# Fused linear attention and SoLU MoE layer on one core: two-bank PSUM rooms with 1024-column instructions, another load order, and a new order of the work

## The chip, the core and the metric

The kernel runs on one core of a Trainium2 chip. The metric is the device time of one execution in microseconds (us). Three runs of the kernel before gave 177.38, 177.45 and 177.94 us; their median, 177.45 us, is what the change is measured against.

## What is computed

The reference takes q, k and v of shape (8 batches, 8 heads, 576 positions, 64 channels) and two weight matrices:

```python
kv  = einsum('bhsd,bhse->bhde', k, v)           # 64x64 per head
o   = einsum('bhsd,bhde->bhse', q, kv)
x   = o / sqrt(mean(o*o, -1) + 1e-6) * g_norm   # then reshaped to (4608 tokens, 512)
h   = x @ w_in                                  # 512 -> 1024
sm  = softmax(h);  u = h * sm
ln  = (u - mean(u)) / sqrt(var(u) + 1e-6) * g_ln
out = ln @ w_out                                # 1024 -> 512
```

The kernel forms u = h * exp(h) without the softmax's denominator, which falls out of the layer norm up to its epsilon; the sum of exp(h) enters through that epsilon alone. The mean over the channels is taken out of w_out beforehand (`w_center`), so a token's output is one matmul times one number per token (`rstd`).

## The kernel before

**Chunks.** The tokens are cut into nine chunks of 512. Chunks 0 to 7 hold eight of the nine positions per row of one batch; chunk 8 (`LAST`) holds the ninth positions of all batches. Each chunk runs through the same stages, and several chunks are in work at once:

- `kv_mm` (L368): k^T v of a batch, 64x64 matmuls on the four quadrants of TensorE (PE), into a PSUM room `kv`; `kv_copy` (L384) copies it to SBUF three times (`part` 0, 1, 2), because the product with q needs it in both partition halves. For batches 0 and 1 the heads come in two groups (second figure 0 or 1 in a piece's name), and the copies are made per group and per pair of heads.
- `qT`: q turned so that the channels lie on the partitions, for chunks 0 to 3 by PE (`qT_mm` L422, eight 128x128 transposes per half, then a copy), for chunks 4 to 8 (`XBAR`) by a DMA transpose that SyncE (SP) issues (`q_turn` L433).
- `o_mm` (L439) in two halves `hf` of four heads each, into two rooms of one bank (z = 0, 1); `sq` (L454) squares on ScalarE (ACT), one instruction of 512 columns per z; `oa` adds the two channel halves; `s_mm` (L462) sums over a head's channels; `ln` and `ex` give the reciprocal root; `x_mul` (L486) on VectorE (DVE) makes x with four instructions of 256 columns per half.
- `h_mm` (L530): eight blocks f of 128 channels, four matmuls (dt = 0 to 3) of 512 columns each, in a room of one bank; `h_exp` (L537) on ACT and `h_u` (L541) on DVE, 512 columns per instruction; `u_sq` (L545) squares u on GpSimd (POOL) or ACT; `e_sum` (L549) on POOL adds the two exponentials of a pair of blocks.
- `fold` (L569) on DVE halves u (`ua`), u squared (`usqa`) and the exponentials' sums (`esa`) `FOLDS` and `E_FOLDS` times; `sums` (L587) adds what is left on PE; `turn`, `stats` and `rstd` make the factor.
- `out_mm` (L649): four token blocks m, eight matmuls each; `scale` (`ob`) multiplies by `rstd`; `store` writes to DRAM. The last block of chunk 8 goes in two halves of 256 columns (L656).

**Order.** Nothing is scheduled by the compiler. `ORDER` (L20) is a list of pieces; `Plan.emit` (L150) issues them in that sequence, so each engine works its own pieces in the order of the list, and waits where an operand or a room is not ready. A suffix such as `:act` names the engine where there is a choice. `ROOMS` (L93) gives for each tile, when it is first used, the number of the PSUM bank or buffer that it gets. `Plan.run` (L122) adds three waits: the next POOL piece waits for DVE's folds and adds that stand before it in the list; a DMA transpose on SP waits for the load before the last one that POOL issued; and the next load that POOL issues waits for the DMA transposes before it.

**Loads.** The second group of k and v of batch 0 comes as fp32 through SP (`wide`) and is narrowed by ACT; all other loads of k, v, q and the weights are issued by POOL, with a cast to bf16. Before, the POOL queue carries q.0.1, v.0.0, k.0.0, q.0.0, v.1.0, k.1.0, q.1.0, w_in.0, w_in.1, q.1.1, v.1.1, k.1.1, w_out.0, w_out.1, q.2.0, k.2.0, v.2.0, q.3.0, v.3.0, k.3.0, q.4.0 and so on. Seven groups of matmuls on zeros (`warm`, L297; 27 in all) stand among the first pieces.

Of the kernel before, what the change touches and what calls it, by code (L numbers as in the profile page):

```python
# [19 lines left out]
ORDER = """  # L20
wide.v ident wide.k g_rows q.0.1 v.0.0 k.0.0 q.0.0 v.0.1:act v.1.0 k.1.0 q.1.0 w_in.0 k.0.1:act w_in.1 warm.0
kv_mm.0.1.0 qT_mm.0.1 kv.0.1.0.0:act kv.0.1.1.0 kv_mm.0.1.1 q.1.1 qT.0.1:act kv.0.1.2.1 kv.0.1.2.0 kv.0.1.1.1
kv.0.1.0.1:act warm.1 kv_mm.0.0.0 v.1.1 kv_mm.0.0.1 o_mm.0.1 kv.0.0.0.1 sq.0.1.1 warm.2 qT_mm.0.0 k.1.1 kv.0.0.1.0:act
kv.0.0.2.0:act kv.0.0.1.1:act kv.0.0.0.0:act qT.0.0 kv.0.0.2.1:act sq.0.1.0 warm.3 o_mm.0.0 w_out.0 turn_g sq.0.0.0
s_mm.0.1 g_mean sq.0.0.1 warm.4 kv_mm.1.0.1 w_out.1 ex.0.1 kv_mm.1.0.0 kv.1.0.2.1 s_mm.0.0 kv.1.0.2.0 kv.1.0.0.1:act
kv.1.0.0.0 kv.1.0.1.1 kv.1.0.1.0 qT_mm.1.0 ex.0.0 q.2.0 qT.1.0:act x.0.0.0 x.0.0.1 warm.5 o_mm.1.0 sq.1.0.0 warm.6
h.0.6.0 h.0.3.0 k.2.0 sq.1.0.1 x.0.1.0 table h.0.0.0 oa.1.0 x.0.1.1 s_mm.1.0 h.0.2.0 h.0.7.0 h.0.2.1 ln.1.0 v.2.0
ex.1.0 h.0.6.1 x.1.0.1 exp.0.6 q.3.0 h.0.3.1 exp.0.2 x.1.0.0 h.0.7.1 h.0.1.0 exp.0.7 u.0.6 v.3.0 qT_mm.1.1 h.0.0.1
exp.0.3 h.0.1.1 u.0.2 usq.0.6 h.1.2.0 exp.0.0 qT.1.1 kv_mm.1.1.1 exp.0.1 kv_mm.1.1.0 k.3.0 kv.1.1.0.1 h.0.4.0 h.0.4.1
u.0.1 kv.1.1.2.1:act kv.1.1.0.0:act es.0.0 kv.1.1.1.0:act kv.1.1.2.0:act kv.1.1.1.1 u.0.3 o_mm.1.1 exp.0.4 h.0.5.0  # L30
u.0.7 sq.1.1.0 es.0.3 h.0.5.1 u.0.4 sq.1.1.1 h.1.0.0 w_mean.0 usq.0.1:act oa.1.1 u.0.0 exp.0.5 s_mm.1.1 ln.1.1 ex.1.1
u.0.5 es.0.2 w_mean.1 w_mean.2 w_mean.3 w_mean.4 w_mean.5 w_mean.6 usq.0.5:act x.1.1.1 usq.0.2 usq.0.7:act w_mean.7
x.1.1.0 usq.0.0 q.4.0 usq.0.4:act w_center.5 h.1.3.0 qT_mm.2.1 h.1.7.0 w_center.1 h.1.4.0 h.1.7.1 qT.2.1:act q.5.0
w_center.4 h.1.0.1 v.4.0 w_center.0 exp.1.7 qT_mm.2.0 exp.1.0 w_center.3 h.1.1.0 h.1.1.1 k.4.0 qT.2.0:act w_center.2
h.1.2.1 es.0.1 u.1.7 h.1.3.1 exp.1.1 h.1.4.1 u.1.0 exp.1.3 out.0.2.0 es.1.0 usq.0.3 u.1.1 exp.1.2 out.0.2.1 kv_mm.2.0
w_center.7 exp.1.4 h.1.5.0 w_center.6 kv.2.1.0:act kv.2.0.0:act h.1.5.1 kv.2.0.2:act kv.2.1.1 kv.2.0.1:act es.1.1
u.1.4 out.0.2.2 kv.2.1.2:act exp.1.5 o_mm.2.0 u.1.3 o_mm.2.1 sq.2.0.1 out.0.2.3 usq.1.1 u.1.2 qT_mm.3.0 sq.2.0.0 u.1.5
out.0.0.0 sq.2.1.1 oa.2.0 out.0.0.1 sq.2.1.0 qT.3.0 s_mm.2.0 usq.1.5 out.0.0.2 ln.2.0 qT_mm.3.1 oa.2.1:pool ex.2.0
h.1.6.0 qT.3.1 out.0.0.3 usq.1.2:act x.2.0.0 x.2.0.1 h.1.6.1 s_mm.2.1 exp.1.6 sums.0 usq.1.7 ln.2.1 u.1.6 ex.2.1
kv_mm.3.0 es.1.2 turn.0 stats.0 out.0.3.0 kv.3.1.0:act x.2.1.0 x.2.1.1 usq.1.0:act out.0.3.1 usq.1.4 usq.1.3 h.2.6.0  # L40
out.0.3.2 rstd.0 h.2.0.0 ob.0.0:act usq.1.6 kv.3.0.1 ob.0.2 h.2.6.1 kv.3.1.2:act kv.3.0.0:act kv.3.1.1:act out.0.3.3
usqa.1.0 kv.3.0.2:act h.2.4.0 exp.2.6 h.2.5.0 ob.0.3:act ua.1.0 o_mm.3.0 h.2.1.0 store.0.3 sq.3.0.0 h.2.0.1 sq.3.0.1
u.2.6 h.2.1.1 store.0.0 exp.2.0 h.2.5.1 usqa.1.1 out.0.1.0 exp.2.1 oa.3.0 h.2.4.1 ua.1.1 exp.2.5 qT.4 s_mm.3.0
out.0.1.1 u.2.0 ln.3.0 es.1.3 out.0.1.2 u.2.5 h.2.7.0 ex.3.0 h.2.7.1 u.2.1 exp.2.4 es.2.0 h.2.3.0 x.3.0.1 exp.2.7
o_mm.3.1 sq.3.1.0 x.3.0.0 usq.2.6 out.0.1.3 sq.3.1.1 h.2.2.0 h.2.3.1 u.2.7 qT.5 ob.0.1:act h.2.2.1 oa.3.1 sums.1
exp.2.3 u.2.4 es.2.3 kv_mm.4.0 exp.2.2 u.2.3 store.0.1 usq.2.5:act s_mm.3.1 turn.1 es.2.2 out.1.3.0 kv.4.1.0
kv.4.0.1:act ln.3.1 u.2.2 store.0.2 out.1.3.1 kv.4.0.0 usq.2.7 ex.3.1 stats.1 out.1.2.0 kv.4.0.2:act kv.4.1.1 kv.4.1.2
rstd.1 x.3.1.1 usq.2.0 o_mm.4.0 o_mm.4.1 ob.1.3 sq.4.0.1 out.1.0.0 usq.2.4 x.3.1.0 sq.4.0.0 store.1.3 out.1.2.1
sq.4.1.0 oa.4.0 ua.2.0 sq.4.1.1 s_mm.4.0 out.1.0.1 ln.4.0 oa.4.1 h.3.2.0 ex.4.0 ob.1.0 v.5.0 s_mm.4.1 x.4.0.0 h.3.7.0
k.5.0 ln.4.1 x.4.0.1 exp.3.2 es.2.1 h.3.3.0 ex.4.1 u.3.2 h.3.6.0 exp.3.3 ua.2.1 exp.3.7 h.3.5.0 x.4.1.0 u.3.3 v.6.0  # L50
exp.3.6 x.4.1.1 h.3.1.0 exp.3.5 q.6.0 usq.2.2:act h.3.4.0 usq.3.3 ob.1.2:act usq.2.1:act usq.2.3:act exp.3.4 es.3.1
# [684 lines left out]
```

## Time and profile before

| what | value |
| --- | --- |
| median of three runs | 177.45 us |
| span of the profiled execution, first to last instruction | 175.8 us |
| profiled execution's own time | not listed apart; its span is 1.65 us less than the median |
| busy: PE, weight loads, DVE, ACT, POOL | 164.2, 80.3, 145.5, 152.1, 99.8 us |
| granted TensorE clock | 1.00 in every slice |
| first h matmul, end of the last output matmul | 19.84 and 172.5 us |

The span counts from the first instruction to the last. The profile has a page with busy times, groups of instructions and the chain that ended last; the trace behind it answers for a window of time, for one tile, and as a timeline in which runs of like instructions are merged (start, duration, engine, line, operation, how many, and in brackets how long the engine sat idle before it and what ended that). In the timeline, a merged row's duration runs from the first start to the last end.

### The profile page before, as it was taken

Reading aid. Unit: us, or ns where it says so; the run is one execution under the profiler, and the core shown is the slowest. Engines: PE = TensorE matmul, PEld = TensorE weight load, DVE = VectorE, ACT = ScalarE, POOL = GpSimd, SP = SyncE. Lnnn points to the kernel's source line nnn. Section 1 sums busy time; section 2 is a strip of 40 time slices with the busy share of each in tenths; the row PEclk is TensorE's granted clock in tenths of the full one; section 3 lists DMA queues with packets and bytes.
Section 4 is the critical chain, followed back from the end, with each engine's and each line's share of the span. In section 5 each row is a group of like instructions: output and inputs, shape, how many; then the busy total and the mean of one; then the engine's idle time right before and its main releaser. Section 6 shows DMA issues by size and latency. Waiting matters only on the chain.

```text
span 175.8 us, 4843 instructions
## 1 busy us (share of the span) xinstructions
PE 164.2 (93%) x1913; PEld 80.3 (46%) x1938; DVE 145.5 (83%) x317; ACT 152.1 (86%) x273; POOL 99.8 (57%) x108
## 2 busy tenths in 40 slices
...
GB/s 179 218 203 214 206 275 373 209 208 208 208 210 210 218 210 129 127 206 235 205 183 259 150 52 193 156 73 93 195 206 105 5 118 126 2 60 93 196 213 159
DMA packets 34623, 30.27 MB, mean 172 GB/s; under 512 B 16288, under 2 KB 28328, under 8 KB 34600
## 3 DMA queue, kind: packets, MB, share of 16 engines
...
q10 hardware_dynamic: 432, 0.66, 1.0%
q8 instruction: 15, 0.25, 0.6%
q14 instruction: 8, 0.07, 0.1%
HBM read 32.51 MB, written 9.44 MB: 239 GB/s over the span
## 4 chain that ended last, share of the span: by engine, by line
PE 75%; DVE 10%; ACT 5%; DMA 5%; issue 2%; POOL 1%; POOLq 0%; DVEq 0%; ACTq 0%
PE h_ps L532 31%; PE out_ps L651 30%; DMA k_sb<-in_k_dram 5%; PE kv_ps L375 4%; PE o_ps L448 3%; DVE u_sb L543 3%; PE sum_ps L594 3%; PE s_ps L465 3%; DVE x_sb L489 2%; DVE w_out_sb L638 2%; ACT osq_sb L233 2%; DVE osq_sb L460 1%; PE out_ps L659 1%; ACT e_sb L539 1%; ACT kvd L229 1%
## 5 line engine op out<-in xcount | busy, mean ns | idle before, releaser
L532 PE MATMUL h_ps<-x_sb,w_in_sb 128*128 128x512 bf16 x280 | 68.0, 379 | 0.5
L651 PE MATMUL out_ps<-w_out_sb,u_sb 128*128 128x512 bf16 x266 | 65.2, 379 | 0.7 <-issue 0.3
L551 POOL TENSOR_TENSOR es_sb<-e_sb 128x512 bf16<-128x512 f32 x36 | 45.4, 1279 | 33.5 <-ACT e_sb L539 13.0
L539 ACT ACTIVATE e_sb<-h_ps,zero_t 128x512 f32<-128x512 f32 x72 | 46.2, 690 | 2.3 <-PE h_ps L532 1.7
L543 DVE TENSOR_TENSOR u_sb<-h_ps,e_sb 128x512 bf16<-128x512 f32 x72 | 46.6, 684 | 1.3 <-ACT e_sb L539 1.0
L532 PEld LDWEIGHTS <-w_in_sb 128*128 128x128 bf16 x288 | 27.3, 98 | 32.5 <-issue 1.3
L651 PEld LDWEIGHTS <-u_sb 128*128 128x128 bf16 x280 | 26.4, 98 | 31.6 <-issue 1.0
L233 ACT ACTIVATE usq_sb<-u_sb,zero_t 128x512 bf16<-128x512 bf16 x49 | 33.6, 718 | 0.0
L489 DVE SCALAR_TENSOR_TENSOR x_sb<-o_ps,g_sb,rst_sb 128x256 bf16<-128x256 f32 x72 | 30.2, 478 | 3.1 <-ACT rst_sb L476 2.5
L235 POOL TENSOR_TENSOR usq_sb<-u_sb 128x512 bf16<-128x512 bf16 x23 | 23.6, 1043 | 7.9 <-DVE osq_sb L460 5.6
L233 ACT ACTIVATE osq_sb<-o_ps,zero_t 128x512 bf16<-128x512 f32 x36 | 22.8, 689 | 3.5 <-PE o_ps L448 3.4
L239 ACT ACTIVATE ob_sb<-out_ps,rstd 128x512 f32<-128x512 f32 x22 | 14.8, 684 | 4.0 <-PE out_ps L651 3.8
L575 DVE TENSOR_TENSOR usq_sb<-usq_sb 128x2048 bf16<-128x2048 bf16 (+2 forms) x20 | 17.0, 848 | 0.6 <-ACT usq_sb L233 0.4
L229 DVE CAST kvd<-kv_ps 64x128 bf16<-64x128 f32 (+3 forms) x26 | 6.4, 256 | 11.2 <-ACT kvd L229 6.5
L241 DVE TENSOR_SCALAR ob_sb<-out_ps,rstd 128x512 f32<-128x512 f32 (+1 forms) x15 | 10.6, 711 | 4.1 <-PE out_ps L659 2.2
L322 POOL DMA_DIRECT2D v_sb<-in_v_dram x9 | 6.8, 757 | 10.1 <-DVE sum_ps L601 2.8
L472 ACT ACTIVATE lss_sb<-s_ps,eps_t 128x512 f32<-128x512 f32 x16 | 11.1, 695 | 1.0 <-PE s_ps L465 0.7
L476 ACT ACTIVATE rst_sb<-lss_sb,zero_t 128x512 f32<-128x512 f32 x16 | 11.5, 722 | 0.4
L375 PE MATMUL kv_ps<-v_sb,k_sb 64*64 64x64 bf16 x576 | 8.0, 194 | 2.8 <-DMA k_sb<-in_k_dram 1.3
L300 PE MATMUL warm_ps<-zeros 128*128 128x512 bf16 x25 | 8.8, 481 | 1.4 <-DVE zeros L255 1.2
L229 ACT CAST kvd<-kv_ps 64x128 bf16<-64x128 f32 (+3 forms) x34 | 8.2, 243 | 2.2 <-PE kv_ps L375 1.5
L375 PEld LDWEIGHTS <-k_sb 64*64 64x64 bf16 x576 | 6.8, 107 | 6.8 <-DMA k_sb<-in_k_dram 2.6
...
## 6 DMA issues: line engine op xcount, KB each, us to landing
...
k_sb<-in_k_dram POOLq DMA_DIRECT2D x6, 576.0 KB, 13.8
v_sb<-in_v_dram POOLq DMA_DIRECT2D x6, 576.0 KB, 13.0
...
```

The source lines that it names most:

```text
L229: nc.scalar.copy(dst, src) if engine == "act" else on[engine].tensor_copy(dst, src)
L233: nc.scalar.activation(out=dst, in_=src, func=AF.Square, bias=zero_t[:, :])
L235: on[engine].tensor_tensor(out=dst, in0=src, in1=src, op=MUL)
L239: nc.scalar.activation(out=dst, in_=src, func=AF.Copy, scale=by)
L375: nc.tensor.matmul(t[64 * y:64 * y + 64, :], T["k", b][rows, n, i, :], T["v", b][rows, n, i, :], start=(i == 0 and (b < 2 or m == 0)), sto ...
L489: nc.vector.scalar_tensor_tensor(out=t[:, 2 * hf + dh, z], in0=T["o", c, hf, z][:, dh], scalar=g_rep[dh], in1=T["rst", c, hf][:, z], op0=M ...
L532: nc.tensor.matmul(bank(("h", c, f), [128, 512])[:, :], w_in_sb[:, dt, f * 128:(f + 1) * 128], T["x", c][:, dt].rearrange("p a b c -> p (a ...
L539: nc.scalar.activation(out=t[:, f % 2, :], in_=T["h", c, f][:, :], func=AF.Exp, bias=zero_t[:, :])
L543: nc.vector.tensor_tensor(out=t[:, f, :], in0=T["h", c, f][:, :], in1=T["e", c, f // 2][:, f % 2, :], op=MUL)
L551: on[engine].tensor_tensor(out=t[:, n, :], in0=e[:, 0, :], in1=e[:, 1, :], op=ADD)
L575: nc.vector.tensor_tensor(out=to[:, 0:n, :], in0=src[:, 0:n, :], in1=src[:, n:2 * n, :], op=ADD)
L651: nc.tensor.matmul(bank(("out", c, m), [128, d_model])[:, :], T["u", c][:, f, m * 128:(m + 1) * 128], w_out_sb[:, f, :], start=(f == 0), s ...
```

## The change

Six things change together.

1. PSUM becomes one tile. `kv`, `o` and `h` get rooms of two neighbouring banks (`width_of`). `exp`, `u` and `usq` work on 1024 columns (a pair of h blocks), `sq` on both z of a half, `x` on 512 columns (one channel half, both z), `kv_copy` on all four pairs of a batch.
2. For batches 0 and 1, `kv_mm` makes each product twice, in both partition halves, on all four quadrants, and two copies of 128 partitions take the place of the six small ones per group.
3. The load of w_in (second half first) stands ahead of all loads of chunk 1, and the first part of chunk 0's h takes channel blocks dt = 2 and 3 (`dts_of`), that is heads 4 to 7, first.
4. q of chunk 3 is turned by DMA (`XBAR` from 3).
5. `FOLDS` is 3 and `E_FOLDS` 1 from chunk 2 on. Squares of u may also run on DVE (`usq.N:dve`, six of them); ACT has 12 and POOL 18, each of 1024 columns, in place of 49 and 23 of 512.
6. `ORDER` and `ROOMS` are new throughout. All 27 matmuls on zeros stand ahead of the first real one.

The core of the diff (order: first lines and last stage):

```diff
 ORDER = """
-wide.v ident wide.k g_rows q.0.1 v.0.0 k.0.0 q.0.0 v.0.1:act v.1.0 k.1.0 q.1.0 w_in.0 k.0.1:act w_in.1 warm.0
-kv_mm.0.1.0 qT_mm.0.1 kv.0.1.0.0:act kv.0.1.1.0 kv_mm.0.1.1 q.1.1 qT.0.1:act kv.0.1.2.1 kv.0.1.2.0 kv.0.1.1.1
...
+warm.4 wide.k wide.v q.0.1 ident v.0.1 q.0.0 warm.2 warm.1 k.0.0 v.0.0 w_in.1 w_in.0 q.1.0 v.1.0 k.1.0 v.1.1 q.1.1
+warm.6 warm.5 k.1.1 w_out.0 warm.3 warm.0 k.0.1:act w_out.1 q.2.0 kv_mm.0.1 kv.0.1.0:act qT_mm.0.1 kv.0.1.1 qT.0.1.0
+qT.0.1.1:act g_rows turn_g qT_mm.0.0 qT.0.0.0 qT.0.0.1 o_mm.0.1 sq.0.1 s_mm.0.1 ex.0.1 kv_mm.0.0 kv.0.0.1 kv.0.0.0:act
+o_mm.0.0 g_mean x.0.1.0 x.0.1.1 sq.0.0 s_mm.0.0 h.0.1.0 k.2.0 ex.0.0 x.0.0.0 x.0.0.1 h.0.0.0 h.0.5.0 h.0.6.0 h.0.7.0
+h.0.0.1 h.0.1.1 h.0.4.0 qT_mm.1.0 qT.1.0.1 v.2.0 k.3.0 table exp.0.0 u.0.0 qT.1.0.0:act h.0.6.1 h.0.7.1 exp.0.3 u.0.3
+h.0.5.1 h.0.4.1 exp.0.2 es.0.2 es.0.3 v.3.0 kv_mm.1.0 h.0.2.0 h.0.2.1 kv.1.0.1:act kv.1.0.0:act o_mm.1.0 u.0.2 sq.1.0
+oa.1.0 h.0.3.0 h.0.3.1 exp.0.1 qT_mm.1.1 qT.1.1.0 s_mm.1.0 ln.1.0 q.3.0 qT.1.1.1 kv_mm.1.1 kv.1.1.0 kv.1.1.1 o_mm.1.1
+w_mean.0 ex.1.0 sq.1.1 x.1.0.1 x.1.0.0 oa.1.1 usq.0.3 w_mean.1 w_mean.2 s_mm.1.1 usq.0.2:act u.0.1 ln.1.1 ex.1.1
+x.1.1.0 es.0.0 h.1.7.0 h.1.6.0 h.1.4.0 h.1.5.0 w_mean.3 w_mean.4 w_mean.5 es.0.1 w_mean.6 x.1.1.1 w_mean.7 w_center.0
+w_center.1 w_center.7 h.1.7.1 h.1.5.1 h.1.4.1 exp.1.2 u.1.2 h.1.6.1 exp.1.3 usq.0.0 qT_mm.2.1 qT.2.1:act usq.0.1
+usq.1.2 h.1.0.0 h.1.0.1 h.1.1.0 h.1.1.1 h.1.2.0 w_center.2 h.1.2.1 qT_mm.2.0 h.1.3.0 exp.1.0 u.1.3 u.1.0 h.1.3.1
+exp.1.1 sums.0 kv_mm.2 qT.2.0:act out.0.3.0 w_center.3 out.0.1.0 turn.0 out.0.3.1 u.1.1 kv.2.2 stats.0 kv.2.1:act
...
+oa.2.1 k.4.0 ua.1.0 ob.0.1 ln.2.0 es.1.0 ex.2.0 out.0.2.0 s_mm.2.1 ln.2.1 ex.2.1 store.0.0 x.2.0.1 qT.3 x.2.0.0
+out.0.2.1 out.0.2.2 out.0.2.3 ob.0.3:act ob.0.2:act x.2.1.0 x.2.1.1 usq.1.0:dve kv_mm.3 kv.3.1 h.2.7.0 q.4.0 h.2.6.0
+kv.3.0:act h.2.3.0 ua.1.1 kv.3.2 h.2.1.0 h.2.6.1 h.2.7.1 exp.2.3 h.2.2.0 q.5.0 h.2.2.1 o_mm.3.0 h.2.3.1 es.1.1 v.4.0
...
+h.7.0.0 ua.6.0 h.7.1.0 exp.7.0 es.7.0 ua.6.1 ua.6.2 x.8.0.1 x.8.0.0 x.8.1.1 x.8.1.0 h.7.7.0 usq.6.2:act ob.5.2 u.7.0
+h.7.6.0 exp.7.3 es.6.1 h.8.0.0 es.6.3 usqa.6.0 store.3.2 store.5.2 h.8.1.0 exp.8.0 u.7.3 h.8.7.0 h.8.5.0 h.8.6.0 u.8.0
+usqa.6.1 usqa.6.2 exp.8.3 es.7.3 h.8.2.0 u.8.3 h.8.3.0 exp.8.1 h.8.4.0 exp.8.2 h.7.3.0 esa.6.0 sums.6 out.6.3.0 es.8.1
+es.8.2 out.6.3.1 es.8.0 h.7.2.0 u.8.1 usq.8.1:act u.8.2 es.8.3 ua.8.0 out.6.1.0 turn.6 stats.6 usq.8.2:act exp.7.1
+rstd.6 ob.6.3:act usq.7.0:dve out.6.0.0 out.6.0.1 usq.8.3:act h.7.5.0 usq.8.0:act out.6.2.0 u.7.1 usq.7.1:dve es.7.1
+out.8.0.0 out.8.2.0 usq.7.3 esa.8.0 ob.6.0 h.7.4.0 exp.7.2 es.7.2 out.6.1.1 store.6.0 usqa.8.0 usqa.8.1 ua.8.1
+out.6.2.1 ua.8.2 usqa.8.2 sums.8 store.6.3 u.7.2 usq.7.2:act out.8.0.1 store.5.1 store.5.3 out.8.2.1 out.8.1.0
+out.8.1.1 turn.8 stats.8 rstd.8 ob.8.0:act store.8.0 ua.7.0 ob.6.2:act store.6.2 usqa.7.0 out.7.1.0 out.5.0.0 out.5.0.1
+out.7.1.1 ua.7.1 ua.7.2 usqa.7.1 ob.8.1:act esa.7.0 usqa.7.2 sums.7 store.8.1:act ob.8.2:act store.8.2:act ob.6.1
+store.6.1 out.7.0.0 out.7.0.1 ob.5.0 store.5.0 turn.7 stats.7 rstd.7 out.8.3.1 out.7.3.0 ob.7.1:act ob.7.0 store.7.1
+store.7.0 ob.8.3.1:act out.7.3.1 ob.7.3:act out.7.2.0 store.7.3 out.7.2.1 store.8.3.1 ob.7.2:act store.7.2 out.8.3.0
+ob.8.3.0:act store.8.3.0:act
 """
...
-    XBAR = tuple(range(4, NC))
-    FOLDS = (0, 2, 2, 2, 2, 3, 3, 3, 3)
-    E_FOLDS = (0, 0, 0, 0, 0, 1, 1, 1, 1)
+    XBAR = tuple(range(3, NC))
+    FOLDS = (0, 2, 3, 3, 3, 3, 3, 3, 3)
+    E_FOLDS = (0, 0, 1, 1, 1, 1, 1, 1, 1)
...
+    def width_of(key):
+        return 2 if key[0] in ("o", "h", "kv") else 1
+
+    psum = ps.tile([128, 8 * 512], FP32, name="psum")
...
+    def kv_mm(b, x):
+        t = bank(("kv", b, x) if b < 2 else ("kv", b), [128, 2, 512])
+        for m in range(2):
+            for i in range(9):
+                for w in range(2):
+                    n = range(NP)[kv_pairs(b, x if b < 2 else w)][m]
+                    for r in range(2):
+                        rows, y = slice(64 * r, 64 * r + 64), r ^ w
+                        nc.tensor.matmul(
+                            t[64 * y:64 * y + 64, w, m * D:(m + 1) * D], T["k", b][rows, n, i, :], T["v", b][rows, n, i, :],
+                            start=(i == 0 and m == 0), stop=(i == 8), skip_group_check=True,
+                        )
...
+    def kv_copy_pair(engine, b, x, w):
+        copy(
+            engine, kvd[b, x, w][:, 0],
+            T["kv", b, x][:, w, 0:2 * D].rearrange("p (m i h) -> p m h i", m=2, h=2),
+        )
...
-    def o_sq(engine, c, hf, z):
+    def o_sq(engine, c, hf):
         t = kept_tile(("osq", c, hf), [128, 2, 2, 256], BF16)
-        square(engine, t[:, :, z, :], T["o", c, hf, z].rearrange("p d y c -> p d (y c)"))
+        square(engine, t.rearrange("p d z c -> p z d c"), T["o", c, hf].rearrange("p z d y c -> p z d (y c)"))
...
+    dts_of = [(2, 3, 0, 1) if c == 0 else tuple(range(NP)) for c in range(NC)]
...
-    def h_exp(c, f):
-        t = kept_tile(("e", c, f // 2), [128, 2, 512], FP32)
-        nc.scalar.activation(out=t[:, f % 2, :], in_=T["h", c, f][:, :], func=AF.Exp, bias=zero_t[:, :])
+    def h_exp(c, n):
+        t = kept_tile(("e", c, n), [128, 2, 512], FP32)
+        nc.scalar.activation(out=t[:, :, :], in_=T["h", c, n][:, :, :], func=AF.Exp, bias=zero_t[:, :])
...
-        nc.vector.tensor_tensor(out=t[:, f, :], in0=T["h", c, f][:, :], in1=T["e", c, f // 2][:, f % 2, :], op=MUL)
+        nc.vector.tensor_tensor(out=t[:, 2 * n:2 * n + 2, :], in0=T["h", c, n][:, :, :], in1=T["e", c, n][:, :, :], op=MUL)
```

270 lines of the change are left out of this document (109 added, 161 removed).

## The prediction

> **What bounds the kernel now.** First I read the page: the busy times, then the chain that ended last.
>
> ```profile
> span 175.8 us, 4843 instructions
> PE 164.2 (93%) x1913; PEld 80.3 (46%) x1938; DVE 145.5 (83%) x317; ACT 152.1 (86%) x273; POOL 99.8 (57%) x108
> ...
> PE 75%; DVE 10%; ACT 5%; DMA 5%; issue 2%; POOL 1%; POOLq 0%; DVEq 0%; ACTq 0%
> ```
>
> PE carries three quarters of the chain. DVE and ACT are nearly as full, so a share alone doesn't decide it. The same sums by stage do, cut at the first h matmul (19.84), at the end of batch 2's kv_mm (41.10) and at the end of the last output matmul (172.55). Behind the stretch and its length stand the busy us of PE, weight loads, DVE, ACT and POOL, the granted clock, the DMA share and GB/s:
>
> ```profile
> 10.00:15.00 5.00, 3.40 (x82) 2.16 (x83) 0.92 (x2) 2.60 (x9) 2.89 (x4) 1.00 1.23 207
> 15.00:19.84 4.84, 4.06 (x71) 2.06 (x71) 3.91 (x13) 3.72 (x7) 1.48 (x2) 1.00 1.12 217
> 19.84:41.10 21.26, 19.23 (x216) 9.95 (x219) 18.17 (x36) 19.88 (x33) 16.73 (x18) 1.00 1.22 255
> 41.10:172.55 131.45, 130.13 (x1496) 62.98 (x1506) 120.37 (x250) 120.99 (x221) 71.45 (x68) 1.00 0.82 155
> ```
>
> Behind 41.10 PE stands idle for 131.45 - 130.13 = 1.32 us only. Ahead of it, it is idle for 2.03 us. What DVE and ACT save can hardly shorten the long stage; PE work taken out, and an earlier start, can. The start is set by loads, as the timeline and the chain say:
>
> ```profile
> 11.26 0.76 PE L375 MATMUL kv_ps<-v_sb,k_sb 64*64 64x64 bf16 x36 [1.31 <-DMA k_sb<-in_k_dram]
> 12.74 0.71 POOL L322 DMA_DIRECT2D k_sb<-in_k_dram  x1 [0.52 <-DMA q_sb<-in_q_dram]
> 17.39 0.62 PE L427 MATMUL qt_ps<-ident,q_sb 128*128 128x128 bf16 x8 [0.55 <-DMA q_sb<-in_q_dram]
> 19.83 0.98 PEld L532 LDWEIGHTS <-w_in_sb 128*128 128x128 bf16 x6 [0.27 <-DMA w_in_sb<-in_moe_w_in_dram]
> 40.40 0.77 PE L375 MATMUL kv_ps<-v_sb,k_sb 64*64 64x64 bf16 x72 [0.51 <-DVE u_sb L543]
> ```
>
> The brackets give landings: q.0.0, the last load of chunk 0, at about 12.7; q.1.0 at 17.4; w_in.0 at 19.8.
>
> **PE work that goes.** The chain prices it by runs of like matmuls:
>
> ```profile
> 12.01 0.42 PE o_ps L448 x16
> 15.09 0.54 PE s_ps L465 x2
> 45.73 0.45 PE qt_ps L427 x8
> 47.86 1.30 PE sum_ps L594 x80
> 119.44 0.56 PE sum_ps L594 x32
> 144.42 4.33 PE h_ps L532 x20
> 158.68 0.34 PE sum_ps L594 x16
> ```
>
> Chunk 3's two groups of eight transposes go: 2 x 0.45 = 0.90 us. With FOLDS 3 and E_FOLDS 1, the sums of chunks 2, 3 and 4 shrink from 32 matmuls to 16: 3 x (0.56 - 0.34) = 0.66 us. Together **-1.56 us**. Both lay in the dense stage. The doubled kv_mm of batches 0 and 1 costs PE nothing: 72 matmuls on four quadrants took 0.77 us (40.40), 36 on two took 0.76 (11.26). Were it not so, the bound is 2 x 0.76 = 1.5 us, on PE alone.
>
> **The head.** In the new load order, w_in.1 and w_in.0 come straight behind chunk 0. One half of w_in takes 19.83 - 17.39 = 2.4 us, so they land at 15.1 and 17.5, and the six loads of chunk 1 end where they did:
>
> ```profile
> 26.60 0.65 PEld L375 LDWEIGHTS <-k_sb 64*64 64x64 bf16 x36 [0.42 <-DMA k_sb<-in_k_dram]
> ```
>
> The order asks k.1.0 for kv_mm.1.0 at about 22, when it lands too (12.7 + 2 x 2.4 + the 4.7 that three loads of chunk 1 took), and k.1.1 at 26.6. The first h is set by chunk 0: v.0.0, now its last load, at 12.7; kv_mm.0.0 0.76; a copy (0.29) and o_mm 0.42; the square on 1024 columns; s_mm 0.54. What the wide instructions cost:
>
> ```profile
> L543 DVE TENSOR_TENSOR u_sb<-h_ps,e_sb 128x512 bf16<-128x512 f32 x72 | 46.6, 684 | 1.3 <-ACT e_sb L539 1.0
> L539 ACT ACTIVATE e_sb<-h_ps,zero_t 128x512 f32<-128x512 f32 x72 | 46.2, 690 | 2.3 <-PE h_ps L532 1.7
> L489 DVE SCALAR_TENSOR_TENSOR x_sb<-o_ps,g_sb,rst_sb 128x256 bf16<-128x256 f32 x72 | 30.2, 478 | 3.1 <-ACT rst_sb L476 2.5 <-ACT rst_sb L482 0.4
> L229 DVE CAST kvd<-kv_ps 64x128 bf16<-64x128 f32 x10 | 2.9, 289 | 1.5 <-PE kv_ps L375 0.9 <-ACT kvd L229 0.3
> L638 DVE SCALAR_TENSOR_TENSOR w_out_sb<-u_sb,g_sb,mean_ps 128x512 bf16<-128x512 f32 x8 | 5.4, 739 | 0.0
> L229 ACT CAST v_sb<-u_sb 128x1152 bf16<-128x1152 f32 x1 | 1.2, 1152 | 2.9 <-DMA u_sb<-in_v_dram 2.9
> L575 DVE TENSOR_TENSOR usq_sb<-usq_sb 128x2048 bf16<-128x2048 bf16 x8 | 9.8, 1219 | 0.4 <-ACT usq_sb L233 0.4
> L575 DVE TENSOR_TENSOR usq_sb<-usq_sb 128x1024 bf16<-128x1024 bf16 x8 | 5.5, 690 | 0.2
> L575 DVE TENSOR_TENSOR usq_sb<-usq_sb 128x512 bf16<-128x512 bf16 x4 | 1.7, 423 | 0.0
> L241 DVE TENSOR_SCALAR ob_sb<-out_ps,rstd 128x512 f32<-128x512 f32 x13 | 9.6, 747 | 1.9 <-ACT rstd L617 1.0 <-PE out_ps L651 0.9
> L601 DVE STREAM_TRANSPOSE sum_ps<-sum_ps 128x128 f32<-128x128 f32 x9 | 2.9, 324 | 1.2 <-PE sum_ps L594 1.1
> L551 POOL TENSOR_TENSOR es_sb<-e_sb 128x512 bf16<-128x512 f32 x36 | 45.4, 1279 | 33.5 <-ACT e_sb L539 13.0 <-DVE usq_sb L575 10.2 <-DVE ua_sb L575 5.8
> ```
>
> On ACT, 1024 columns lie between 0.69 (512) and 1.15 (1152): I take 1.06. On DVE the scalar-tensor-tensor grows by 0.739 - 0.478 = 0.26 per 256 columns: x on 512 is 0.74, u on 1024 is 0.684 + 0.52 = 1.2. So 12.7 + 0.76 + 0.3 + 0.42 + 1.06 + 0.54, and five handovers of some 0.1 to 0.2, make 16.5; on DVE g_mean and the two x of heads 4 to 7 (0.74 each) queue behind the copy of kv.0.0 and end at about 16.8. I take **16.9** for the first h, against 19.84.
>
> That isn't all gain: chunk 1's first half used to be ahead of 19.84 and now comes behind. From the first h to the end of kv_mm.2 the new list holds 64 h matmuls (4.33 / 20 = 0.217 each, 13.9), three kv_mm (2.3), four groups of transposes (1.8), two o_mm (0.84), two s_mm (0.5), eight w_mean, and sums.0 (1.3):
>
> ```profile
> 31.10 1.95 PE L632 MATMUL mean_ps<-u_sb,ua_sb 128*128 128x512 f32 x7
> ```
>
> With w_mean at 8 x 0.25 = 2.0 that is 22.6 us. For the waits in it I take what the same stretch held before, 2.03, and 0.3 for chunk 1's second half, whose copies and squares now stand alone: 16.9 + 22.6 + 2.3 = 41.8. At 41.10 the kernel before had two h blocks (8 matmuls) and sums.0 still to do, but four output matmuls done: 4 x 0.217 + 1.3 = 2.2 us less far. So the head gives 41.10 + 2.2 - 41.8 = **-1.5 us**. With waits of 0.5 it would be -3.3, with 4 us +0.2.
>
> **Chunk 3 by DMA.** Its loads are over when those of before were; its transposes are a new wait:
>
> ```profile
> 27.39 0.80 POOL L322 DMA_DIRECT2D k_sb<-in_k_dram  x1
> k_sb<-in_k_dram POOLq DMA_DIRECT2D x1, 576.0 KB, 21.1
> 57.18 6.24 SPq L435 DMA_TRANSPOSE qT_sb<-q_sb  x2
> DMA to landing us min/median/max: 3.8/4.4/6.9
> ```
>
> 27.4 + 21.1 = 48.5 ends chunk 3's loads, now with q.3.0. SP issues qT.3 behind it and behind store.0.0, at about 48.9; it lands at 53.3 (median) or 55.8 (longest). PE asks for it in o_mm.3.0: behind 41.8 come 32 output and 16 h matmuls (48 x 0.217 = 10.4), two o_mm and two s_mm (1.4) and kv_mm.3 (0.77), so 54.4. The cost is 0 to 1.4; I take **0.4**, near the median. Behind the wait queue q.4.0 on POOL, and with it es.1.1 and v.4.0; kv_mm.4 comes some 11 us behind o_mm.3.0, which covers them.
>
> **DVE and ACT.** exp falls from 46.2 to at most 36 x 1.06 = 38 us, u from 46.6 to 36 x 1.2 = 43. PE waited 1.32 us behind 41.10, so the gain is between 0 and 1.3: I take **-0.3**. The last stage goes the other way. From h.7.0.0 to sums.7 PE has 34 pieces of four matmuls (29.5) and two sums (0.7): 30.2. DVE has in the list there the folds of chunks 6, 7 and 8 (each 2 x (1.22 + 0.69 + 0.42) + 0.69 = 5.35, so 16.0), eight u (9.6), four x (3.0), two squares (1.4), two output scalings (1.5) and two rounds of turn (0.32) and stats' four small ones (about 1 together with it, an estimate from turn's time): 33.5, of which two output pieces' time (1.8) is a head start. That is 1.5 us late, or nothing where instructions overlap as u does (46.6 / 72 = 0.647 against 0.684). I take **+1.0**.
>
> **Sum.** 175.8 - 1.56 - 1.5 + 0.4 - 0.3 + 1.0 = 173.8 us of span. The median lies 177.45 - 175.8 = 1.65 above it, which I add: **175.4 us**. Its own bounds are 173.4 to 177.4.
>
> **Rivals.**
>
> *Two-bank rooms hold PE back (slower).* A pair of h blocks is given free only after exp and u on 1024 columns, 1.06 + 1.2 = 2.3 us behind its last matmul, where one block took 0.69 + 0.68 = 1.4. In the new list nine of 36 h rooms are opened with no more than one PE piece behind the last reader (h.4.6.0 behind u.4.1, h.7.7.0 behind x.8.0.0). If half of the 0.9 us shows in each, PE waits 4 us: **179.4**. It decides from 2 us on. Against it: before, with some twenty such openings, all idleness was 1.32 us.
>
> *The clock falls in the thin head.* Before, zeros fill PE's gaps; now they all come first, and from about 9 to 16.9 PE has some 4.5 us of work. What a low rate is, the start shows:
>
> ```profile
> 1.20 5.29 PE L300 MATMUL warm_ps<-zeros 128*128 128x512 bf16 x14 [1.20 <-DVE zeros L255]
> 5.01 0.15 PEld L300 LDWEIGHTS <-zeros 128*128 128x128 bf16 x1 [0.28 <-issue]
> 5.44 0.55 PEld L300 LDWEIGHTS <-zeros 128*128 128x128 bf16 x3 [0.28 <-issue]
> ```
>
> Weight loads come 0.43 us apart up to 5.44 and closer behind it: half rate for 4.2 us. Again at the first h, that costs 2.1: **177.5**. Against it: PE was busy 3.40 of 5 us from 10 to 15 and kept its rate, and no gap in the new head is over 1.5 us. The Trainium skill (TensorE: Matmul & The Clock Gate, "Why this matters for your kernels") asks for no idle gap over about 3 us; by that rule the rate holds here, as it did in the trace across the 1.31 us ahead of 11.26; only its window of activity, for which it gives no threshold, could still drop it.
>
> *POOL stands in DVE's way at the end.* The two squares on DVE (usq.7.0, usq.7.1) aren't held apart from POOL's work, as the folds are by Plan.run. If each waits for one es (1.28), DVE is 2.6 us later where it already sets the pace: **178.0**. No row shows such an overlap. The Trainium skill (SBUF — State Buffer, "Who interferes with whom") says that a DVE instruction with two SBUF inputs and a POOL instruction that reads SBUF exclude each other, and the first to issue has the port: that would be this case.
>
> *The head and the end run without waits (faster).* 1.8 less in the head, 1.0 less at the end: **172.6**.
>
> **Chances.** The forecast 0.50, rooms 0.18, clock 0.08, POOL 0.06, no waits 0.18. About 0.3% (0.53 us) is what a measurement of this kernel can tell from no change, so faster means below 176.9. Four fifths of the forecast's case and all of the last make 0.58 faster; 0.14 same (0.07, most of the clock's case, part of POOL's); 0.28 slower. The range takes in the second and the last case, 172.3 to 179.6; the forecast's own is 173.4 to 177.4.
>
> **What would show it.** Right: the first h near 16.9; kv_mm.2 ending near 41.8; o_mm.3.0 waiting less than 1.5 us for a DMA; PE idle below 3 us behind it; wide u near 1.2 us and exp near 1.06; sums.7 up to 1.5 us late behind DVE's folds. Wrong: PE waiting in front of h or output matmuls for u, x or ob by more than 2 us in all; h matmuls 0.43 apart behind 16.9; a first h behind 18.5; wide instructions as long as two narrow ones.

## The result and the profile after

Before 177.62 us, after 211.78 us (medians of 4 runs each, 177.38 to 177.94 and 208.56 to 212.21): 1.183 times as long, 95% interval 1.174 to 1.192. The ratios, here and below, compare only the fast runs of both kernels (of the kernel after, those of 208.56 and 211.65 us), while a time in us is the median of all runs. The forecast was 175.4 us with a range of 172.3 to 179.6. The profiled run took 212.21 us, the longest of the four. Its page, with busy times and the chain that ended last:

```profile
span 210.4 us, 4843 instructions
PE 170.4 (81%) x1993; PEld 80.6 (38%) x2018; DVE 166.5 (79%) x238; ACT 128.4 (61%) x170; POOL 119.2 (57%) x105
...
PE 49%; DVE 30%; ACT 7%; DMA 6%; issue 4%; POOL 1%; SPq 0%; DVEq 0%; ACTq 0%; POOLq 0%
```

ACT has 24 us less to do than before. DVE has 21 us more (145.5 before), and its part of the chain went from 10 to 30%. PE stands idle for 40.0 us of the span (210.4 - 170.4), against 11.6 before (175.8 - 164.2). The groups of instructions tell where (busy us, mean ns of one):

```profile
L539 DVE TENSOR_TENSOR u_sb<-psum,e_sb 128x1024 bf16<-128x1024 f32 x36 | 43.3, 1217 | 2.9 <-ACT e_sb L535 2.8
L481 DVE SCALAR_TENSOR_TENSOR x_sb<-psum,g_sb,rst_sb 128x512 bf16<-128x512 f32 x36 | 25.0, 743 | 5.0 <-ACT rst_sb L469 2.9 <-ACT rst_sb L475 2.0
L571 DVE TENSOR_TENSOR ua_sb<-u_sb 128x2048 bf16<-128x2048 bf16 x8 | 14.4, 1806 | 0.1
L453 DVE TENSOR_TENSOR osq_sb<-osq_sb 128x512 bf16<-128x512 bf16 x13 | 11.9, 916 | 1.7 <-ACT osq_sb L231 1.6
L571 DVE TENSOR_TENSOR usq_sb<-usq_sb 128x2048 bf16<-128x2048 bf16 x8 | 11.4, 1424 | 0.1
L571 DVE TENSOR_TENSOR es_sb<-es_sb 128x1024 bf16<-128x1024 bf16 x7 | 9.4, 1346 | 1.4 <-POOL es_sb L547 1.4
L571 DVE TENSOR_TENSOR usq_sb<-usq_sb 128x512 bf16<-128x512 bf16 x7 | 9.2, 1319 | 0.1
L535 ACT ACTIVATE e_sb<-psum,zero_t 128x1024 f32<-128x1024 f32 x36 | 39.7, 1114 | 20.5 <-PE psum L528 14.7 <-DVE u_sb L539 2.6 <-POOL usq_sb L233 2.5
```

The wide u and x cost what the prediction took (1.2 and 0.74 us), exp a little more (1.11 against 1.06). The adds with both inputs in SBUF, the folds and the add of the squares of o, cost up to three times their price: 1806 ns against 1219 before, 1319 against 423. Summed instruction by instruction, as what each VectorE instruction took over the lower quartile of its shape, this excess is 28.6 us, against 1.4 before. One case, an add of the squares of o (`oa`), in the timelines of DVE, POOL and PE:

```profile
63.61 4.75 DVE L453 TENSOR_TENSOR osq_sb<-osq_sb 128x512 bf16<-128x512 bf16 x1
```

```profile
60.75 1.52 POOL L320 DMA_DIRECT2D q_sb<-in_q_dram  x2 [4.80 <-DMA qT_sb<-q_sb]
62.28 1.29 POOL L547 TENSOR_TENSOR es_sb<-e_sb 128x512 bf16<-128x512 f32 x1
63.51 0.78 POOL L320 DMA_DIRECT2D v_sb<-in_v_dram  x1
64.31 3.76 POOL L233 TENSOR_TENSOR usq_sb<-u_sb 128x1024 bf16<-128x1024 bf16 x2
```

```profile
68.41 0.38 PE L458 MATMUL psum<-osq_sb,head_mean 128*128 128x512 bf16 x1 [4.11 <-DVE osq_sb L453]
```

POOL stood 4.8 us on q.4's load, which waits for chunk 3's DMA transposes, and only then did its two wide squares. The add on DVE, 0.43 us elsewhere, ended when they had ended, and PE waited 4.11 us for it. The longest wait of PE has another beginning: three folds that cost 1.22 + 0.69 + 0.42 us undisturbed took 8.32 us beside three sums and a wide square of POOL, u stood behind them, and o_mm waited for the PSUM room that u had still to read.

```profile
126.65 8.32 DVE L571 TENSOR_TENSOR usq_sb<-usq_sb 128x2048 bf16<-128x2048 bf16 x3
```

```profile
136.50 0.65 PE L441 MATMUL psum<-qT_sb,kvd 64*32 64x256 bf16 x16 [6.69 <-DVE u_sb L539]
```

Such waits of PE, in the list of waits (us in all, how many, the longest):

```profile
PE psum L441 <- DVE u_sb L539: 9.5, 2, 6.7
PE psum L458 <- DVE osq_sb L453: 8.0, 4, 4.1
PE psum L590 <- DVE ua_sb L571: 3.4, 2, 3.0
PE psum L647 <- DVE u_sb L539: 2.4, 1, 2.4
```

These are 23.3 us. The 9.5 of o_mm are waits for a room: it is through the rooms too that DVE's lateness reaches PE. The granted clock falls as well, in the head (first row) and in or behind such a wait (the other two; 0.87 from 70 to 80). What that costs beyond the waits wasn't separated. Three stretches, with length, PE, weight loads, DVE, ACT, POOL, and behind the counts the granted clock, DMA share and GB/s:

```profile
10.00:20.00 10.00, 6.57 (x123) 3.35 (x126) 4.95 (x10) 5.74 (x7) 3.79 (x6) 0.72 1.14 210
...
60.00:70.00 10.00, 5.37 (x37) 2.45 (x39) 8.69 (x6) 5.38 (x6) 8.79 (x8) 0.95 0.91 145
...
130.00:140.00 10.00, 3.17 (x37) 1.40 (x38) 9.81 (x13) 2.80 (x5) 8.41 (x6) 0.70 0.50 96
```

### The profile page after: what moved, and what is told of

It is laid out like the page before. It is cut to its first block, busy times and chain, and to the rows that moved or that the text cites. A ratio compares the mean times of both kernels' runs of the same rounds, so it can differ in the third digit from the quotient of the medians.

```text
span 210.4 us, 4843 instructions
## 1 busy us (share of the span) xinstructions
PE 170.4 (81%) x1993; PEld 80.6 (38%) x2018; DVE 166.5 (79%) x238; ACT 128.4 (61%) x170; POOL 119.2 (57%) x105
## 4 chain that ended last, share of the span: by engine, by line
PE 49%; DVE 30%; ACT 7%; DMA 6%; issue 4%; POOL 1%; SPq 0%; DVEq 0%; ACTq 0%; POOLq 0%
PE psum L647 18%; PE psum L528 17%; DVE usq_sb L571 8%; DVE u_sb L539 7%; DVE osq_sb L453 4%; DMA qT_sb<-q_sb 4%; PE psum L298 4%; DVE es_sb L571 3%; PE psum L441 3%; DVE ua_sb L571 3%; DMA out_dram<-ob_sb 3%; ACT osq_sb L231 2%; ACT e_sb L535 2%; PE psum L458 2%; PE psum L590 2%
## 5 line engine op out<-in xcount | busy, mean ns | idle before, releaser
L647 PE MATMUL psum<-w_out_sb,u_sb 128*128 128x512 bf16 x264 | 67.3, 394 | 4.2 <-DVE u_sb L539 2.4
L528 PE MATMUL psum<-x_sb,w_in_sb 128*128 128x512 bf16 x281 | 69.0, 390 | 1.9 <-ACT ob_sb L237 0.7
L535 ACT ACTIVATE e_sb<-psum,zero_t 128x1024 f32<-128x1024 f32 x36 | 39.7, 1114 | 20.5 <-PE psum L528 14.7
L233 POOL TENSOR_TENSOR usq_sb<-u_sb 128x1024 bf16<-128x1024 bf16 x18 | 35.1, 1962 | 20.4 <-DVE usq_sb L571 7.9
L539 DVE TENSOR_TENSOR u_sb<-psum,e_sb 128x1024 bf16<-128x1024 f32 x36 | 43.3, 1217 | 2.9 <-ACT e_sb L535 2.8
L231 ACT ACTIVATE osq_sb<-psum,zero_t 128x1024 bf16<-128x1024 f32 x18 | 19.8, 1114 | 16.8 <-PE psum L441 8.3
L481 DVE SCALAR_TENSOR_TENSOR x_sb<-psum,g_sb,rst_sb 128x512 bf16<-128x512 f32 x36 | 25.0, 743 | 5.0 <-ACT rst_sb L469 2.9
L237 ACT ACTIVATE ob_sb<-psum,rstd 128x512 f32<-128x512 f32 (+1 forms) x28 | 18.2, 669 | 5.1 <-PE psum L647 2.6
L231 ACT ACTIVATE usq_sb<-u_sb,zero_t 128x1024 bf16<-128x1024 bf16 x12 | 13.4, 1140 | 5.3 <-DVE u_sb L539 5.3
L571 DVE TENSOR_TENSOR ua_sb<-u_sb 128x2048 bf16<-128x2048 bf16 x8 | 14.4, 1806 | 0.1
```

The lines of the kernel that those rows point to most:

```text
L231: nc.scalar.activation(out=dst, in_=src, func=AF.Square, bias=zero_t[:, :])
L233: on[engine].tensor_tensor(out=dst, in0=src, in1=src, op=MUL)
L237: nc.scalar.activation(out=dst, in_=src, func=AF.Copy, scale=by)
L481: nc.vector.scalar_tensor_tensor(out=t[:, 2 * hf + dh].rearrange("p z a b -> p z (a b)"), in0=T["o", c, hf][:, :, dh].rearrange("p z a b - ...
L528: nc.tensor.matmul(bank(("h", c, f // 2), [128, 2, 512])[:, f % 2, :], w_in_sb[:, dt, f * 128:(f + 1) * 128], T["x", c][:, dt].rearrange(" ...
L535: nc.scalar.activation(out=t[:, :, :], in_=T["h", c, n][:, :, :], func=AF.Exp, bias=zero_t[:, :])
```

## The experiments

**Theories.** Five were tried. 1: POOL's tensor work holds off DVE's adds with two SBUF inputs, and PE waits for DVE. Rivals: 2, the rooms of two banks or the wide instructions; 3, the fall of the clock in the head upsets the order; 4, chunk 3's turn by DMA; 5, the order itself, whatever the durations.

### The disputed cost by itself

The kernel leaves the computation out and holds only rows of VectorE and GpSimd instructions.

> This kernel leaves the whole computation out and measures one cost by itself: six VectorE instructions of each kind (the add on 128x512 and the fold on 128x2048, both with two SBUF inputs; the square on 1024 columns; u on 1024 and x on 512, each with one input in PSUM; the output scaling), each once with GpSimd idle and once beside a gapless row of GpSimd squares on 1024 columns, on 512 columns, and of its f32 sums on 512. Theory 1 (GpSimd's tensor work holds VectorE's two-SBUF-input instructions off): the adds and squares take 0.43, 1.22 and about 0.7 us alone and several times that beside GpSimd, one of them up to the length of one or two GpSimd instructions (2 to 4 us beside squares on 1024); u, x and the scaling keep their 1.22, 0.74 and 0.75. If the width of GpSimd's square is what matters, the adds beside squares on 512 are held about half as long. Rival theories (2: rooms of two banks; 3: the clock; 4: chunk 3's transposes) put the long adds down to something else: the adds here stay within 0.1 us of their time alone.

VectorE's groups by stage: the fold with GpSimd idle; the fold and the 512 add beside GpSimd's f32 sums; u beside its wide squares; x beside its narrow ones.

```profile
L62 DVE TENSOR_TENSOR ua<-u 128x2048 bf16<-128x2048 bf16 x6 | 7.4, 1225 | 2.7 <-POOL pes L80 2.5
...
L80 POOL TENSOR_TENSOR pes<-pe 128x512 bf16<-128x512 f32 x8 | 15.3, 1907 | 0.5
L62 DVE TENSOR_TENSOR ua<-u 128x2048 bf16<-128x2048 bf16 x6 | 13.1, 2183 | 5.6 <-POOL pd L78 5.4
...
L60 DVE TENSOR_TENSOR osq<-osq 128x512 bf16<-128x512 bf16 x6 | 8.5, 1478 | 5.4 <-POOL pd L78 5.4
...
L66 DVE TENSOR_TENSOR d<-psum,e 128x1024 bf16<-128x1024 f32 x7 | 8.6, 1224 | 0.2
...
L69 DVE SCALAR_TENSOR_TENSOR xt<-psum,one,e 128x512 bf16<-128x512 f32 x6 | 4.5, 751 | 5.4 <-POOL pd L76 5.2
```

Beside the sums the add goes from 0.42 to 1.48 us, the fold from 1.23 to 2.18 (2.80 beside the wide squares), and GpSimd's sum from 1.27 to 1.91. u and x, with one input in PSUM, and the output scaling don't change. One expectation failed: beside the wide squares the six short adds kept their 0.42 us (more in the last section). So the cost is real, and it falls on both engines. The Trainium skill (SBUF — State Buffer, "Who interferes with whom") says just this: two SBUF inputs on VectorE and a read of SBUF by GpSimd exclude each other. These rows agree: of VectorE's instructions only those with two SBUF inputs grew longer.

### Undoing one thing in the kernel after

All 18 squares of POOL to ACT (`usq.0.3` becomes `usq.0.3:act`, and so on):

> All 18 squares on 1024 columns that GpSimd held go to ScalarE (18 x 1.14 = 20.5 us more on it, 35.3 us less on GpSimd). Theory 1: the excess of VectorE's adds over their usual durations falls from 28.6 to below 12 us (the sums of exp stay on GpSimd) and the time from 211.8 to 185-197 us. Theories 2, 3 and 4: nothing they name is touched, and ScalarE has more to do: 208-220 us, with PE waiting for u, x or ScalarE as before.

Measured 212.42 us, ratio 1.195 (1.190 to 1.200). The excess did fall, to 12.5 us, but nothing was won. DVE and POOL were relieved and ACT, now at 145.8 us, was late in their place: PE's waits for ACT are 12.5 us in all, against 4.5 in the kernel after. For theory 1 as I had put it, this is a miss.

Fillers in the head, that is more matmuls on zeros: `warm.7` (4) ahead of s_mm.0.1, `warm.8` (1) ahead of o_mm.0.0, `warm.9` (5) ahead of s_mm.0.0.

> Ten more matmuls on zeros in the three gaps of the thin head (4 ahead of s_mm.0.1, 1 ahead of o_mm.0.0, 5 ahead of s_mm.0.0), all else as in the kernel after. Theory 3 (the fall of the clock upsets the order that was worked out ahead, and the rest follows): the granted clock from 10 to 20 us goes from 0.72 to 1.00, h matmuls from 17 us on are 0.22 apart, and the time falls below 195 us. Theories 1, 2 and 4: the clock is mended too, but only the 2.5 us that it cost come back, 207-212 us.

Chunk 3's turn back on PE (the last two lines are words of `ORDER`):

```diff
-    XBAR = tuple(range(3, NC))
+    XBAR = tuple(range(4, NC))
-qT.3
+qT_mm.3.0 qT.3.0:act qT_mm.3.1 qT.3.1:act
```

> Chunk 3's q is turned on PE again (two groups of eight transposes in place of qT.3, their copies on ScalarE). Theory 4 (the DMA transposes of chunk 3 hold q.4's load on GpSimd for 4.8 us, which bunches GpSimd's squares behind it, and o_mm.3.0 for 1.9): the stall from 60 to 70 us, PE busy 5.4 of 10, goes, and the time falls by over 8 us, to below 203. Theory 1: the first long stall is milder, 3-6 us are won, 205-209 us. Theories 2 and 3: 0-3 us, 209-213 us.

208.01 us (ratio 1.158, 1.152 to 1.165) and 208.45 (1.179, 1.172 to 1.187). The fillers give some 4 us. The turn gives 3.3 us by the medians and 0.7 by the ratios; its interval meets that of the kernel after. Both together:

> The two repairs of the first series together: the ten fillers in the head and chunk 3's q turned on PE. It is the base of the runs below. Alone they gave some 3 to 4 us each. If the fall of the clock or chunk 3's transposes (theories 3 and 4) start a chain of lateness, both gone should do more than the sum, below 200 us; if each is a loss of its own, 203-207 us.

207.8 us (1.166, 1.160 to 1.172), excess still 26.5 us. Theories 3 and 4 explain 3 to 4 us of 34. This kernel is the base of what follows.

exp and u as two instructions of 512 columns:

```diff
-        nc.scalar.activation(out=t[:, :, :], in_=T["h", c, n][:, :, :], func=AF.Exp, bias=zero_t[:, :])
+        for x in range(2):
+            nc.scalar.activation(out=t[:, x, :], in_=T["h", c, n][:, x, :], func=AF.Exp, bias=zero_t[:, :])
...
```

> On the same base, exp and u as two instructions on 512 columns each, in the same rooms of two banks and in the same order: ScalarE gets about 36 x 0.27 = 10 us more, VectorE 36 x 0.15 = 5 us more, and u of the first block no longer waits for exp of the second. Theory 2 in its part on wide instructions: u and the rooms come earlier, and the time falls by over 5 us. Theory 1: VectorE is the one that PE waits for, and the time rises by 2-6 us. Theories 3 to 5: within 3 us of the base.

209.47 us (1.169, 1.167 to 1.172), 1.7 above the base by the medians and 0.5 by the ratios. The width of exp and u isn't the cause. Theory 1 isn't helped either: it had expected 2 to 6 us more.

### POOL's tensor work thinned out

> On that base, GpSimd's 18 squares take 32 of 512 columns and its 36 sums of exp 64 of 512 (most of this work is left out; the tiles hold constants there), so GpSimd is never late and holds nobody off; every instruction, wait and room is otherwise as it was, and ScalarE gets nothing more to do. Theory 1 (GpSimd's tensor work holds VectorE's adds off, and VectorE's lateness is what PE waits for): the excess of VectorE's adds falls from 26 to about 0-2 us, VectorE to about 138 us, and the time to 176-186 us. Theory 2 (the rooms of two banks): PE's waits stay, 197-206 us. Theory 5 (the order itself leaves PE without work, whatever the durations): 195-205 us.

> As the run with thin GpSimd work, and VectorE's folds take 32 of 512 columns too (the sums are then not those of the reference): VectorE is relieved of some 35 us more. Theory 1: little more is to be had, 0-5 us below that run. A sixth reading, that VectorE's own work is too much for this order even undisturbed: 5-15 us below it. Theories 2 and 5: still above 190 us.

201.96 and 200.24 us, but neither decides anything. The tiles that POOL no longer fills had to hold constants, and writing these ahead of everything delayed the first matmul from 1.20 to 14.03 us. Without that delay (in the sums of exp 64 columns likewise; squares and sums lie in fixed buffers there):

```diff
+        cols = slice(0, 32 if engine == "pool" and ("usq", c) not in firsts else 512)
-        square(engine, t[:, 2 * n:2 * n + 2, :], T["u", c][:, 2 * n:2 * n + 2, :])
+        square(engine, t[:, 2 * n:2 * n + 2, cols], T["u", c][:, 2 * n:2 * n + 2, cols])
...
```

> The run with thin GpSimd work again, without the constants that were written ahead of the first matmul (there the warm matmuls began at 14.03 us where they begin at 1.20 in the kernel after, so some 13 us of its 202 were the experiment's own). The first chunk in each of the two rooms of squares and sums of exp is computed whole; from then on GpSimd's squares take 32 of 512 columns and its sums 64 (that work is left out). Theory 1 (GpSimd's tensor work holds VectorE's adds off): 183-190 us, VectorE's excess below 4 us, against 207.8 for its base. Theory 2 (rooms) and 5 (order): 198 us or more, since they explain the loss without GpSimd.

188.4 us (185.97, 186.75, 190.06 and 191.39), 19.4 below the base, as theory 1 said. Page and two groups of the profiled run:

```profile
span 185.0 us, 4920 instructions
PE 169.9 (92%) x2044; PEld 80.7 (44%) x2044; DVE 142.6 (77%) x238; ACT 129.7 (70%) x172; POOL 71.7 (39%) x105
...
L463 DVE TENSOR_TENSOR osq_sb<-osq_sb 128x512 bf16<-128x512 bf16 x13 | 6.1, 465 | 1.8 <-ACT osq_sb L241 1.6
L583 DVE TENSOR_TENSOR usq<-usq 128x2048 bf16<-128x2048 bf16 x8 | 9.7, 1217 | 0.1
```

The adds are nearly back at their old prices (excess 4.1 us) and DVE has 142.6 us, near the 166.5 - 28.6 = 137.9 that the kernel after would have without the excess. Work is missing here, so these 19.4 us are what POOL's tensor work costs in this order by all its ways: the stretched adds, and POOL's own lateness. The two aren't told apart here. PE's waits for DVE, summed over the span (1.2 us each time are the zeros at the start), go the same way: 2.6 us before, 25.3 after, 23.7 in the base and 7.0 here.

> As the run before, and the folds of VectorE take 32 of 512 columns too, except in the first chunk of each room (that work is left out). If VectorE's own undisturbed work is still the bound: 5 us or more below the run with thin GpSimd work. If only its disturbance was: within 3 us of it. What is then left above the 175 us forecast belongs to rooms and order.

192.46 us (two runs, 190.89 and 194.02): DVE with 119.5 us gains nothing more. It is even 4 us slower, outside what was expected, and why stays open. Undisturbed, DVE isn't the bound.

What is left for the rooms shows in PE's waits with thin POOL work:

```profile
PE psum L468 <- DVE osq_sb L463: 3.1, 3, 1.6
...
PE psum L430 <- DVE ob_sb L249: 1.2, 1, 1.2
PE psum L451 <- DVE u_sb L549: 1.2, 2, 0.9
PE psum L659 <- ACT ob_sb L247: 1.1, 1, 1.1
```

Only the last three can be rooms that came free late: 3.5 us in all. That holds where DVE is on time; a run of the new order with rooms of one bank is missing.

### Fewer adds, other hands, and a wait in place of the disturbance

```diff
-    FOLDS = (0, 2, 3, 3, 3, 3, 3, 3, 3)
-    E_FOLDS = (0, 0, 1, 1, 1, 1, 1, 1, 1)
+    FOLDS = (0, 2, 2, 2, 2, 2, 2, 2, 2)
+    E_FOLDS = (0, 0, 0, 0, 0, 0, 0, 0, 0)
```

> On the base with fillers and chunk 3 on PE: two folds per sum for every chunk and none of the sums of exp, so 21 adds of VectorE go (14 on 512 columns, 7 on 1024; about 11 us undisturbed, and the disturbance that fell on them, some 13 us) and PE gets 16 more matmuls in each of seven sums (0.33 each, 2.3 us). Theory 1: 8-15 us faster than the base, 192-200 us. Theories 2 and 5: PE's own work and its waits for rooms stay, 206-211 us.

199.85 us (1.117, 1.110 to 1.124): 8 below the base though PE has more to do, excess 17.3 us. This is the fastest version of the new order that computes everything.

> The kernel with fewer folds (199.9 us) with all 23 squares that GpSimd and VectorE still had on ScalarE, so that of GpSimd's tensor work only the sums of exp and three small adds are left; the whole computation is kept. Theory 1: VectorE's excess falls from 17 to 5-9 us and the time to 190-196 us, unless ScalarE, with 26 us more, becomes the one that is waited for: then 198-206 us, as in the run where it got 18 squares and nothing was won.

211.89 us (1.195, 1.191 to 1.199), above both ranges. (It was 24 squares, 18 of POOL and 6 of DVE.) The excess is 6.6 us and still 12 us are lost: the squares now stand in ACT's queue ahead of exp and the chain of s, and DVE waits for these, as its longest waits show:

```profile
DVE u_sb L540 <- ACT e_sb L536: 19.0, 18, 3.3
...
DVE x_sb L482 <- ACT rst_sb L470: 12.8, 9, 2.5
```

Both engines kept apart in both directions, on the base:

```diff
+            if name[0] in ("usq", "es", "oa"):
+                self.sums.append(ins)
...
             self.adds.append(ins)
+            self.after(ins, self.sums[-1:])
```

> The base with fillers and chunk 3 on PE, and one more order: an add of VectorE also waits for the last GpSimd sum or square that stands ahead of it in the list (so far only GpSimd waits for the adds ahead of it). The two never overlap then. If being caught by a later GpSimd instruction is a large part of the disturbance: the adds are back at 0.42, 0.69 and 1.22 us and the time falls to 198-204 us. If the adds only wait for what holds them anyway, the waits take the place of the stretching: 205-212 us.

231.37 us (1.303, 1.300 to 1.307), 23.6 above the base and far above both ranges. No add is stretched any more (excess 1.7 us), and DVE waits instead:

```profile
DVE ua_sb L576 <- POOL es_sb L552: 19.4, 5, 5.6
DVE usq_sb L576 <- POOL es_sb L552: 11.0, 4, 5.5
...
DVE usq_sb L576 <- POOL usq_sb L238: 4.8, 2, 2.8
```

So keeping the two apart by waits is dearer than the overlap: POOL's instruction, which the list has ahead of the add, is often not done when DVE comes to the add.

### The same in the kernel before

```diff
         if engine == "pool":
-            self.after(ins, self.adds)
             self.adds.clear()
```

> The kernel before with one thing changed: GpSimd's instructions no longer wait for VectorE's adds that stand ahead of them in the list (these waits order the engines and guard no data). Theory 1: adds and GpSimd's squares and sums overlap, VectorE's excess rises from 1.4 to 10-25 us, and the time by 3-15 us, to 181-193. If such overlap costs VectorE little, or PE doesn't wait for it: within 1 us of 177.5, or faster.

185.99 us (1.049, 1.047 to 1.051): 8.7 us, with an excess of 13.4 us. The group of folds on 512 columns had 423 ns before:

```profile
L574 DVE TENSOR_TENSOR usq_sb<-usq_sb 128x512 bf16<-128x512 bf16 x4 | 3.6, 896 | 0.0
```

And PE waits for the adds of the squares of o, 0.7 us in all before:

```profile
PE s_ps L464 <- DVE osq_sb L459: 4.3, 6, 1.7
```

The mechanism of theory 1 is thus shown in the old order too, where only these waits were taken out.

### Two parts of the change alone, in the kernel before

`qT.3` in place of `qT_mm.3.0`, the other three pieces out:

> The kernel before with one part of the change alone: chunk 3's q turned by DMA, asked for where the first group of transposes stood. By the prediction's own terms: two groups of eight transposes go (-0.9 us on PE), the landing costs 0 to 1.4 us; 176.5-178 us. A reading by which the transposes hold GpSimd's loads, and through them VectorE's adds, in any order: 179-183 us.

186.95 us (1.053, 1.050 to 1.055), above both ranges. PE waited 7.2 us at o_mm.3.0. By Plan.run a turn waits for the last load but one ahead of it in the list. Here that is v.4.0, and SP issued the turn at 56.38 us only:

```profile
61.27 0.64 PE L447 MATMUL o_ps<-qT_sb,kvd 64*32 64x256 bf16 x16 [7.17 <-DMA qT_sb<-q_sb]
```

That price was of the place I gave it, so a second try puts `qT.3` behind k.3.0 and `k.4.0 v.4.0 q.4.0 q.5.0` behind usq.1.6:

> The kernel before with chunk 3's q turned by DMA, the turn right behind the load of k.3.0 in the list and the four loads of chunks 4 and 5 moved behind it, behind GpSimd's last squares of chunk 1 (in the first try the turn waited for v.4.0, was issued at 56.38 us and PE waited 7.2 us for it). If the turn's own price is what the prediction took (0 to 1.4 us against 0.9 us of PE work saved): 176.3-178 us, with o_mm.3.0 waiting less than 1.5 us. If the waits between loads and turns make it dear wherever it stands: 180-187 us.

184.63 us (1.039, 1.037 to 1.042). Chunk 3's own wait is gone, and chunk 4 pays, whose loads come later here:

```profile
53.51 0.42 PE L447 MATMUL o_ps<-qT_sb,kvd 64*32 64x256 bf16 x16
...
70.58 1.17 PE L447 MATMUL o_ps<-qT_sb,kvd 64*32 64x256 bf16 x32 [4.15 <-DMA qT_sb<-q_sb]
```

`ua.c.2`, `usqa.c.2` and `esa.c.0` added for chunks 2, 3 and 4 with FOLDS 3 and E_FOLDS 1:

> The kernel before with another part alone: three folds and one fold of the sums of exp for chunks 2, 3 and 4 too. By the prediction: 3 x (0.56 - 0.34) = 0.66 us less on PE, 176.8 us. Theory 1: nine more adds on VectorE (3 x (2 x 0.42 + 0.69) = 4.6 us), which GpSimd waits for or which it disturbs, while VectorE was busy 92% of that stage: 178-182 us.

> Both parts together in the kernel before. By the prediction -1.56 + 0.4, 176.3 us; by theory 1 the sum of the two costs, 179-184 us.

179.99 us (1.014, 1.012 to 1.016) and 189.03 (1.065, 1.061 to 1.069). Both parts make the old order slower, and together, with the turn in its first place, by about their sum. That is above the 179 to 184 expected, since the turn alone had cost more than either reading gave it. With the folds alone the excess stays at 1.3 us, so here they aren't stretched; whether they cost by their own time or by waits wasn't separated. No version found beats the kernel before.

## Why the prediction was wrong

**The step that failed** is the one on DVE and ACT, -0.3 behind 41.10 and +1.0 for the last stage. It took the long stage to be as free of waits as in the old order, summed u and exp, and left the adds at the prices of the old trace. These prices held only while POOL kept clear of them. With 28.6 us more on the adds DVE became the engine that PE waits for: 25.3 us in all, 2.6 before. Thinning POOL's work gives 19.4 of the 34 us back. How much of that is the stretched adds and how much POOL's own lateness no run separates; with the squares off POOL the excess fell to 12.5 us and nothing was won, since ACT was late instead.

**The rival "POOL stands in DVE's way"** had the mechanism, with a chance of 0.06 and a price of 2.6 us. Two of its sentences were wrong. The folds are not held apart from POOL's work by Plan.run: POOL waits for adds ahead of it in the list, but an add doesn't wait for a POOL instruction that is late. And "no row shows such an overlap" wasn't so. One was there in the kernel before, in the timelines of DVE and POOL:

```profile
30.23 0.79 DVE L460 TENSOR_TENSOR osq_sb<-osq_sb 128x512 bf16<-128x512 bf16 x1
```

```profile
28.21 2.52 POOL L551 TENSOR_TENSOR es_sb<-e_sb 128x512 bf16<-128x512 f32 x2
```

0.79 in place of 0.43, beside two sums.

**PE work that goes** (-1.56) was counted rightly: sums of 16 matmuls take 0.34 (sums.7, 197.54 to 197.88). As a gain it failed: the folds that buy part of it cost the old order 2.3 us, the turn that buys the rest more still.

**The head.** The first h (its weight load) came at 17.1 us against 16.9 forecast. kv_mm.2 ended at 44.71, not 41.8. With the fillers alone, the clock held, it ended at 43.19, so some 1.5 us were the clock and 1.4 the waits, which were set too low. Against the 43.3 (41.10 + 2.2) of the old order that is a gain of 0.1 us, not 1.5.

**The rival on the clock** did occur in the profiled run. Weight loads of h came 0.43 us apart until 21.36:

```profile
17.12 0.15 PEld L528 LDWEIGHTS <-w_in_sb 128*128 128x128 bf16 x1 [0.28 <-issue]
17.55 0.15 PEld L528 LDWEIGHTS <-w_in_sb 128*128 128x128 bf16 x1 [0.28 <-issue]
...
20.96 0.15 PEld L528 LDWEIGHTS <-w_in_sb 128*128 128x128 bf16 x1 [0.28 <-issue]
```

No idle time of PE ahead of it was over 1.25 us, so the Trainium skill's rule (TensorE: Matmul & The Clock Gate, "Why this matters for your kernels") against gaps over about 3 us was kept here, and the clock fell all the same. In the profiles of two other kernels with the same thin head (all squares on ACT; chunk 3 on PE) the clock stayed at 1.00 from 10 to 20 us. So the fall belongs to some executions and not to the order alone, and with the fillers' 4 us at most it is a small part of the 34.

**Chunk 3 by DMA** (+0.4). PE waited 1.89 us, over the bound of 1.4. The work queued behind q.4.0 on POOL was named, and its cover was sought in kv_mm.4 alone. What it hit was an add on DVE (63.61). In the new order undoing it is worth at most some 3 us. In the old order the two places tried cost 9.3 and 7.2 us, by waits between loads and turns; the second price is that of the four moved loads too.

**DVE in the last stage** (+1.0). The wait came at sums.8, not at sums.7, which stood without one: 2.95 us for a fold, twice the 1.5 that the sum gave. Chunk 8's folds were stretched too (esa.8.0 took 2.38 us for 0.69).

```profile
189.91 0.24 PE L590 MATMUL psum<-ua_sb,stat_sel 128*32 128x128 bf16 x4 [2.95 <-DVE ua_sb L571]
```

**Rooms.** The rival's sign did show: PE waited in front of h and output matmuls for u, x or ob 3.6 us (2.4 + 0.5 + 0.7), and 9.5 in front of o_mm for a room. With POOL's work thin, at most 3.5 us of rooms are left, so here they mostly passed DVE's lateness on. How much narrower rooms would have spared wasn't tried. The doubled kv_mm cost nothing (0.78 us).

**Open.** What makes POOL late in the new order isn't settled; q.4.0's wait is one case. Of the 11 us between the kernel with thin POOL work and the one before, the fillers' work is 2.2 (10 x 0.217) and the waits for rooms at most 3.5; the rest wasn't separated. That the list was laid out for durations that the chip doesn't keep is a guess that no run tried.
